# The first half of the fourth 1/den load, moved ahead of three LN2 transposes in the DMA queue

## Chip, cores, metric

One NeuronCore of one Trainium2 chip. The metric is the device time of one execution in microseconds (us).

## The reference, cut

One transformer block on 2048 tokens of width 1024: a modulated layernorm, a linear attention with 32 heads, a second modulated layernorm (LN2) and a GEGLU feed-forward network (FFN) of width 3584. What matters here:

```python
num = einsum(pq, kv);  den = einsum(pq, z) + 1e-6
o = num / den                                   # 1/den per token and head
x = x + ga * (o @ wo)                           # "x1"
h = layernorm(x) * (1 + cb) + sb                # LN2
x = x + gb * ((gelu(h @ w_gate) * (h @ w_up)) @ w_down)
```

## The kernel before

Tokens go in 16 tiles of 128, in four groups of 512. The 1/den of a group is computed once, stored to DRAM and loaded back spread over partitions: two halves for each group, each of four loads of 256 KB. The queries `pq` are multiplied by it on VectorE, then TensorE makes the attention output of one tile after another (`wo_chunk`). Groups share two buffers, so the fourth group's load overwrites the second's.

```python
def rb_load(sg, hs=(0, 1)):
    i = sg % 2                                   # buffer
    for h in hs:
        for k in range(HPG):                     # four loads of 256 KB
            sch.dma(Q, ... RB[i][32*k:32*(k+1), h] <- scr_rd[sg, h, k] ...)
...
def ln2_a(c_, late):                             # LN2 of one tile (cut)
    ln_stats_act(c_, b_, rng, 0); ln_stats_act(c_, b_, rng, 1)
    xhat_act(c_, b_, rng)                        # ScalarE: normalized tile
    tdma(Q, H2[sg][...], b_[:, :], ...)          # DMA transpose into h2T
...
ln2_a(0, False)
stream_pair(0, 0)                                # FFN weights: gate, up (512 KB each)
for c_ in range(3, 12):
    if c_ == 3: pq_scale(1, 0, GH[0] + GH[1])
    if c_ == 4: pq_scale(1, 1, GH[0] + GH[1])
    wo_chunk(c_, 2 * (c_ % 4))
    ...
    if c_ == 9:
        stream_pair(0, 1)
        rb_load(3, (1,))
        x_dma(12, 16)
    if c_ in (10, 11): pq_scale(3, 0, GH[c_ - 10])
    if c_ in (4, 5, 6): ln2_a(c_ - 3, False)     # tiles 1, 2, 3
    if c_ == 6: rb_load(3, (0,))                 # <- this moves
    if c_ == 9: mod2(0, 2); mod2(2, 2)           # VectorE: scale and shift of h2T
stream_pair(0, 2)
```

All these DMAs are issued by one engine, SP, in program order; SP waits before each for whatever that DMA needs. The first FFN matmuls need a modulated block of h2T from all four tiles 0 to 3. Tiles count from 0: the transposes of tiles 1, 2 and 3, called transposes 1, 2 and 3, are those of the second, third and fourth tile.

## Time and profile before

| | before |
|---|---|
| median of 3 runs (range), us | 834.2 (833.83 to 834.79) |
| span of the profiled execution, us | 832.2 |
| TensorE busy | 99% |
| third up-weights: issued, landed, us | 238.58, 252.44 |
| TensorE hole there (start to start less the usual 0.216) | 0.588 us |
| first FFN matmul, us | 234.42 |

The first 190 us jitter between executions. Where tenths matter I therefore count from the start of the first attention-output matmul (191.22 us here): "to the end" is the end of the span less that start, 641.00 us in this profile. Steps between matmul starts and DMA landings are from the trace's own instruction and semaphore records; the views print durations and rounded starts.

### The profile page before, as it was taken

The page shows a single profiled execution, that of the slowest core. Times are in us where ns is not written, and L with a number is a line of the kernel's source. Part 1 is how long each engine was busy: PE and PEld are TensorE (multiplying, and loading weights), DVE is VectorE, ACT ScalarE, POOL GpSimd, SP SyncE. Part 2 cuts the span into 40 slices and gives each one's busy share as a digit, 9 for nine tenths or more (in the row PEclk, how much of TensorE's full clock was granted, in tenths as well). Part 3 has the DMA queues.
Part 4 walks back from the last instruction along what each step waited for, and adds up shares of the span by engine and source line. Part 5 has one row for each costly group of instructions (what it writes and reads, how often), then busy time and mean ns, then how long its engine had stood idle before and what let it go on. Part 6 is the DMA issues. An engine that isn't in the chain of part 4 may idle for free.

```text
span 832.2 us, 11518 instructions
## 1 busy us (share of the span) xinstructions
PE 821.7 (99%) x4179; PEld 391.9 (47%) x4253; DVE 509.7 (61%) x920; ACT 321.3 (39%) x542; POOL 36.2 (4%) x90
## 2 busy tenths in 40 slices
PE   8999999999999999999999999999999999999998
PEld 4444446665444444444444444444444444444445
DVE  6799888834776577753555565355556535555522
ACT  2597642323523354410444441044444104444300
POOL 2122200000200000000000000000000000000000
PEclk9999999999999999999999999999999999999999
DMA  9788769358999789170555533065553306555000
GB/s 288 230 182 223 166 136 274 48 121 195 205 254 289 227 244 262 31 173 19 158 153 152 151 102 76 20 163 152 154 146 102 76 20 171 155 152 137 7 20 26
DMA packets 216929, 121.90 MB, mean 146 GB/s; under 512 B 69276, under 2 KB 206756, under 8 KB 215848
## 3 DMA queue, kind: packets, MB, share of 16 engines
q1 hardware_dynamic: 216856, 121.16, 56.1%
q8 instruction: 34, 0.56, 0.3%
q14 instruction: 23, 0.19, 0.1%
q10 hardware_dynamic: 16, 0.00, 0.0%
HBM read 103.03 MB, written 4.47 MB: 129 GB/s over the span
## 4 chain that ended last, share of the span: by engine, by line
PE 92%; SPq 3%; DMA 3%; issue 1%; DVE 1%; ACT 0%; ACTq 0%
PE ps_all L1359 23%; PE ps_all L1334 22%; PE ps_all L1331 21%; PE ps_all L826 7%; PE ps_all L862 7%; PE ps_all L811 5%; PE ps_all L1193 5%; DMA wu<-in_B_w_up_dram 2%; SPq L568 1%; DMA wmq<-in_w_mod_dram 1%; SPq L1172 1%; SPq L573 1%; PE ps_all L844 0%; PE ps_all L1121 0%; SPq L562 0%
## 5 line engine op out<-in xcount | busy, mean ns | idle before, releaser
L1334 PE MATMUL ps_all<-h2T,wu 128*128 128x512 bf16 x896 | 339.6, 379 | 2.3 <-DMA wu<-in_B_w_up_dram 0.4
L1331 PE MATMUL ps_all<-h2T,wg 128*128 128x512 bf16 x860 | 325.9, 379 | 0.0
L1359 PE MATMUL ps_all<-wd,yT 128*128 128x512 bf16 (+3 forms) x934 | 193.1, 366 | 0.9
L1342 ACT ACTIVATE q<-ps_all 128x512 f32<-128x512 f32 x112 | 66.9, 597 | 222.3 <-PE ps_all L1331 217.1
L1359 PEld LDWEIGHTS ps_all<-wd,yT 128*128 128x128 bf16 x952 | 90.1, 98 | 103.7 <-issue 0.2
L1334 PEld LDWEIGHTS ps_all<-h2T,wu 128*128 128x128 bf16 x896 | 87.7, 98 | 106.5 <-DMA wu<-in_B_w_up_dram 0.9
L1331 PEld LDWEIGHTS ps_all<-h2T,wg 128*128 128x128 bf16 x896 | 87.7, 98 | 105.6
L1347 DVE SCALAR_TENSOR_TENSOR ww<-th,guh 128x512 f32<-128x512 f32 x112 | 77.5, 692 | 77.9 <-ACT th L1346 77.9
L1344 DVE SCALAR_TENSOR_TENSOR ww<-q,ps_all 128x512 f32<-128x512 f32 x112 | 76.9, 687 | 74.5 <-ACT guh L1343 74.3
L1346 ACT ACTIVATE th<-ww 128x512 f32<-128x512 f32 x112 | 70.5, 629 | 87.5 <-DVE ww L1344 87.5
L1364 DVE TENSOR_TENSOR ps_all<-ps_all,gbb 128x512 f32<-128x512 f32 (+3 forms) x34 | 22.7, 667 | 94.6 <-PE ps_all L1359 94.6
L1349 DVE TENSOR_TENSOR yT<-ww,ps_all 128x512 bf16<-128x512 f32 x112 | 76.9, 686 | 3.8
L1343 ACT ACTIVATE guh<-ps_all 128x512 f32<-128x512 f32 x112 | 66.3, 592 | 0.0
L862 PE MATMUL ps_all<-h1T,wq 128*128 128x512 bf16 x256 | 56.7, 379 | 0.0
L1193 PE MATMUL ps_all<-w,pq 128*128 128x512 bf16 x252 | 56.3, 379 | 0.2
L811 PE MATMUL ps_all<-wk,h1T 128*128 128x512 bf16 x239 | 55.3, 379 | 1.2 <-DMA wk<-in_A_wqkv_dram 0.5
L800 ACT ACTIVATE eb<-ps_all 128x512 f32<-128x512 f32 x64 | 36.4, 593 | 38.1 <-PE ps_all L811 14.8
L862 PEld LDWEIGHTS ps_all<-h1T,wq 128*128 128x128 bf16 x256 | 25.0, 98 | 29.9
L1193 PEld LDWEIGHTS ps_all<-w,pq 128*128 128x128 bf16 x256 | 24.9, 98 | 30.0 <-ACT w L1123 0.3
L811 PEld LDWEIGHTS ps_all<-wk,h1T 128*128 128x128 bf16 x248 | 23.6, 97 | 28.9 <-DVE h1T L691 2.3
L826 PE MATMUL ps_all<-xall,pk 128*128 128x342 bf16 (+1 forms) x216 | 35.2, 307 | 0.0
L630 ACT ACTIVATE xhd<-xall,nm,rs 128x1024 bf16<-128x1024 bf16 x12 | 14.9, 1240 | 38.2 <-DVE nm L620 31.7
(97 smaller groups left out, 506.6 us busy)
## 6 DMA issues: line engine op xcount, KB each, us to landing
wg<-in_B_w_gate_dram SPq DMA_DIRECT2D x56, 512.0 KB, 3.9
wu<-in_B_w_up_dram SPq DMA_DIRECT2D x56, 512.0 KB, 5.2
rb<-scr_rd SPq DMA_DIRECT2D x32, 256.0 KB, 5.8
wd<-in_B_w_down_dram SPq DMA_DIRECT2D x7, 1024.0 KB, 8.9
wmst<-in_w_mod_dram SPq DMA_DIRECT2D x6, 1024.0 KB, 6.4
wmq<-in_w_mod_dram SPq DMA_DIRECT2D x8, 512.0 KB, 7.5
out_dram<-xall SPq DMA_DIRECT2D x31, 128.0 KB, 1.7
xall<-in_A_x_dram SPq DMA_DIRECT2D x3, 1024.0 KB, 9.1
```

What stands on the lines that cost most here:

```text
L811: o = sch.op(T, lambda e, dc=dc: e.matmul(PS(bank), H1[sg][:, ci, dc, :], W_[:, dc, jg * 512:(jg + 1) * 512], start=(dc == 0), stop=(dc == ...
L826: o = sch.op(T, lambda e, c_=c_: e.matmul(PS(bank, 0, n), PK[c_][:, g * P:(g + 1) * P], xrow(c_, o_, o_ + n), start=(c_ == 0), stop=(c_ == ...
L862: o = sch.op(T, lambda e, dc=dc: e.matmul(PS(b), WQ[:, dc, qc * P:(qc + 1) * P], H1[sg][:, :, dc, :], start=(dc == 0), stop=(dc == NDC - 1 ...
L1193: last[half] = sch.op(T, lambda e, g=g, half=half: e.matmul(PS(b0 + half), PQ[sg][:, g, ci * P:(ci + 1) * P], W2[:, g, half * 512:(half + ...
L1331: og = sch.op(T, lambda e, dc=dc: e.matmul(PS(bg), WG[slot][:, dc, e_ * P:(e_ + 1) * P], H2[sg][:, dc, :], start=(dc == 0), stop=(dc == ND ...
L1334: ou = sch.op(T, lambda e, dc=dc: e.matmul(PS(bu), WU[slot][:, dc, e_ * P:(e_ + 1) * P], H2[sg][:, dc, :], start=(dc == 0), stop=(dc == ND ...
L1342: sch.op(A, lambda e: e.activation(Q1[j][:, :], PS(bg), ACTF.Square, scale=math.sqrt(GELU_A)), prd=pr(bg), wr=rq, note=f"q1 {fc}")
L1344: sch.op(V, lambda e: e.scalar_tensor_tensor(WW[j][:, :], Q1[j][:, :], 1.0, PS(bg), op0=ALU.add, op1=ALU.mult), rd=rq, prd=pr(bg), wr=rw, ...
L1346: sch.op(A, lambda e: e.activation(TH[j][:, :], WW[j][:, :], ACTF.Tanh, scale=GELU_C), rd=rw, wr=rt, note=f"th {fc}")
L1347: sch.op(V, lambda e: e.scalar_tensor_tensor(WW[j][:, :], TH[j][:, :], 1.0, GUH[j][:, :], op0=ALU.add, op1=ALU.mult), rd=rt + rg, wr=rw, n ...
L1349: sch.op(V, lambda e: e.tensor_tensor(YT[:, fc, :], WW[j][:, :], PS(bu), ALU.mult), rd=rw, prd=pr(bu), wr=r_yt(fc), note=f"yT {fc}")
L1359: o = sch.op(T, lambda e, b=b, fc=fc, c0=c0, c1=c1, n=n: e.matmul(PS(b, 0, n), YT[:, fc, ci * P:(ci + 1) * P], WDT[fc // 4][:, fc % 4, c0:c1],
```

## The change

Its intent: issue the half-load earlier, while the queue still has nothing to wait for. It now precedes the transposes of tiles 1, 2 and 3 instead of following them.

```diff
             if c_ == 4:
                 pq_scale(1, 1, GH[0] + GH[1])
+                rb_load(3, (0,))
             wo_chunk(c_, 2 * (c_ % 4))
...
             if c_ in (4, 5, 6):
                 ln2_a(c_ - 3, False)
-            if c_ == 6:
-                rb_load(3, (0,))
```

## The prediction

> **What bounds the kernel now.** I read the busy shares first, then the chain that ended last, then who made TensorE wait between 170 and 300 us (the stretch that the change touches), then the order of time of TensorE, the DMA queue (SP) and VectorE there, and last the DMA share in slices of 2 us.
>
> ```profile
> PE 821.7 (99%) x4179; PEld 391.9 (47%) x4253; DVE 509.7 (61%) x920; ACT 321.3 (39%) x542; POOL 36.2 (4%) x90
> PE 92%; SPq 3%; DMA 3%; issue 1%; DVE 1%; ACT 0%; ACTq 0%
> ```
>
> TensorE is the bound: 99% busy and 92% of the last chain. From 24 us to the end it issues one 128x512 matmul about every 216 ns. A change can help only where TensorE has a hole. The waits of TensorE from 170 to 300 us are one line, and the order of time shows the place:
>
> ```profile
> PE ps_all L1334 <- DMA wu<-in_B_w_up_dram: 0.4, 1, 0.4
> ...
> 251.69 0.38 PE L1331 MATMUL ps_all<-h2T,wg 128*128 128x512 bf16 x1
> 252.49 0.39 PE L1334 MATMUL ps_all<-h2T,wu 128*128 128x512 bf16 x1 [0.42 <-DMA wu<-in_B_w_up_dram]
> 252.72 0.38 PE L1331 MATMUL ps_all<-h2T,wg 128*128 128x512 bf16 x1
> ```
>
> The first up-matmul of the third FFN weight pair starts 804 ns after its predecessor (start times in the trace) instead of 216: 588 ns are lost. The other odd steps of this stretch, 432 ns every 10.79 us, are exactly two steps and recur to the end, so I take them for missing records. The chain says what stands behind the hole:
>
> ```profile
> 220.28 8.42 SPq L670 DMA_TRANSPOSE h2T<-xh  x3
> 228.79 1.94 SPq L1172 DMA_DIRECT2D rb<-scr_rd  x4
> 230.83 0.39 SPq L1271 DMA_DIRECT2D wg<-in_B_w_gate_dram  x1
> 231.32 0.53 SPq L1272 DMA_DIRECT2D wu<-in_B_w_up_dram  x1
> 231.90 5.56 SPq L1172 DMA_DIRECT2D rb<-scr_rd  x4
> 237.50 0.42 SPq L562 DMA_DIRECT2D xall<-in_A_x_dram  x1
> 238.03 0.45 SPq L1271 DMA_DIRECT2D wg<-in_B_w_gate_dram  x1
> 238.58 5.05 SPq L1272 DMA_DIRECT2D wu<-in_B_w_up_dram  x1
> ```
>
> This is the DMA queue: three LN2 transposes (tiles 1 to 3), the four loads that the change moves, second weight pair, second half of the fourth 1/den load, x, third weight pair. Its last load is issued at 238.58 and lands 13.9 us later, at 252.4. In the trace's semaphore records 15 of its 16 increments come at 250.88 to 250.99 and the last at 252.44: one DMA engine was held by a 16 KB instruction fetch that starts at 243.78 and takes 1.36 us. Yet the DMA engines had a hole of their own earlier (last two columns: DMA share, GB/s):
>
> ```profile
> 224.00:226.00 2.00, 2.00 (x11) 0.88 (x9) 1.74 (x2) 0.65 (x2) 1.03 (x3) 1.00 1.27 285
> 226.00:228.00 2.00, 2.00 (x11) 0.94 (x10) 0.97 (x3) 1.24 (x1) 0.13 (x1) 1.00 0.04 8
> 228.00:230.00 2.00, 2.00 (x11) 0.93 (x10) 2.00 (x6) 0.00 (x0) 0.00 (x0) 1.00 1.04 120
> ```
>
> At 226 to 228 us they stand still: the queue is blocked by the fourth transpose's wait for its normalized tile,
>
> ```profile
> SPq L1476 <- ACT xh L630: 2.7, 1, 2.7
> ```
>
> and all behind it waits along, though the moved load has been ready since 207.7 us, when the last scaling that reads its old buffer ends on VectorE.
>
> **What the Trainium skill says.** "DMA: Bandwidth & Descriptors", section "Queues, rings and completion order": each DMA engine consumes descriptors in ring order. The trace agrees: landings of this queue come in issue order. The same page, "Rules for kernel authors": a transpose next to ordinary DMAs needs nothing, so I expect no draining around the transposes; in the trace the packets of the first transpose overlap those of x and of the first weight pair between 218 and 221 us. "Perfetto Trace Analysis", section "DMA Instruction — HWDGE (DVE, Sync)": the window shown for a DMA instruction is descriptor generation, not movement. The trace agrees: the last load above shows 5.05 us and lands after 13.9. "DMA: Bandwidth & Descriptors", "Why a DMA increments its semaphore by 16 and not by 1": only the full 16 means landed, which is why the one late engine at 252.44 counts.
>
> **The change part by part.** Four loads of 256 KB (1 MB) move in the DMA queue from behind transpose 3 to ahead of transpose 1. No instruction of TensorE, VectorE, ScalarE or GpSimd changes its place: the kernel's reordering step covers an earlier segment. Nothing is added.
>
> Costs on the DMA engines, from packets and landings before: the four loads land 1.2 us apart (232.71, 233.96, 235.12, 236.32), so 4.7 us for all four; a weight pair takes 3.6 us; a transpose about 1 us.
>
> Forward from the landing of the first weight pair, 224.9, unchanged: the moved loads land until 224.9 + 4.7 = 229.6. Transposes 1 and 2 landed at 225.7 and 226.5 and now land near 230.6 and 231.4. Transpose 3 is still ready only after its tile at 227.4, and landed at 231.27; it now stands behind a busy queue and lands near 232.4, about 1.1 us later: 4.7 us of added load less the hole, the issue delay behind it and the load no longer sharing engines with it.
>
> Who needs it: VectorE modulates 8 blocks for tiles 0 and 1, then 8 for tiles 2 and 3:
>
> ```profile
> 228.85 2.13 DVE L691 TENSOR_SCALAR h2T<-h2T,cb1T,sbT 128x256 bf16<-128x256 bf16 x8
> 231.37 2.14 DVE L691 TENSOR_SCALAR h2T<-h2T,cb1T,sbT 128x256 bf16<-128x256 bf16 x8 [0.39 <-DMA h2T<-xh]
> ```
>
> The first eight move to about 230.7 to 232.8 (transpose 1), the second to 232.8 to 235.0. The first FFN matmul starts at 234.42 and needs one modulated block of all four tiles: ready at 232.8 + 0.3 = 233.1, so 1.3 us remain of a slack that was 2.8. VectorE makes a block in 0.27 us and TensorE uses one in 0.43, so later blocks stay ahead. This beginning costs nothing. The x1 addition of tile 10 follows at about 235.0 to 236.2; its banks are wanted at 241.3 by the third hidden block. The scaling that waited 1.8 us for the moved load at 236.44 waits no longer and VectorE catches up by 240.
>
> Behind transpose 3 the queue is 3 us or so ahead: second pair 236.1 (before 239.9; wanted at about 241), second half of the load 240.9, x 243.5, third pair 247.2, with the 1.45 us of the fetch 248.7. That is 3.7 us before 252.4 and 3.2 before TensorE wants it (251.69 + 0.22 = 251.9). I keep 2.5 to 3.7 as my range for the advance; 0.6 suffices. The hole of 0.588 us closes. Sum: 834.2 - 0.6 = 833.6. All after it runs at TensorE's pace with no other DMA wait, so the gain is kept but cannot grow: the other 3 us that the DMA gains meet no waiting engine.
>
> **The rivals.** First: the transposes come too late and the hole moves to 234.42. SP's issue may be blocked by a full queue (the first half-load at 231.90 needed 4.16 us, and transpose 1 2.67). If transposes 2 and 3 are issued only when the moved loads are nearly done, near 228.7, transpose 3 lands at 228.7 + 3.8 = 232.5: still in time. If transpose 1 lands 1.5 us later than I say, each further us costs nearly one: 834.2 to 835.2. For it speaks the saturated queue; against it the 1.3 us of slack. Chance 15%.
>
> Second: the load is hidden either way and the third pair lands no earlier, as SP is blocked elsewhere: 834.2. Its issue waits are back-pressure, which an emptier queue reduces, so I give it 10%.
>
> Third: a large gain, as the DMA queue is full for 40 us. Against it: TensorE lost only 0.588 us to DMA here, and this is the ceiling unless the trace hides more. Under 2%.
>
> Fourth: the earlier second pair lets TensorE start the FFN sooner. No: it issues the last attention-output matmul immediately before 234.42, without a gap.
>
> **Range and chances.** Centre 833.6. The three runs before span 833.83 to 834.79, about half a us to either side, as large as the effect. With the gain and that scatter 832.9 to 834.1; with the first rival up to 834.6. I say 832.9 to 834.6. Over 2% would be 16.7 us; nothing here is of that size. Faster 0.5%, same 99%, slower 0.5%.
>
> **What would show it.** Right: no DMA wait of TensorE near 252; start to start there back at 216 ns; the 226 to 228 slice full of 8 KB packets (220 GB/s instead of 8); transpose 3 landing at 232 to 233; second modulation starting near 232.8; third up-weights landing before 250; VectorE's waits for the 1/den load down from 6.0 us to about 4.2; span near 831.6. Wrong: a TensorE wait on VectorE's modulation at 234.4, or transpose 3 landing after 234, or the up-weight wait still there.

## The result, and the profile after

| | before | after |
|---|---|---|
| median, us, 6 runs each | 833.95 | 833.83 |
| range, us | 833.53 to 834.79 | 833.48 to 835.07 |
| ratio, 95% interval | | 1.000 (0.9987 to 1.0012) |
| profiled span, us | 832.2 | 832.4 |
| first attention-output matmul to the end, us | 641.00 | 640.61 |

A ratio is the mean time of one kernel's fast runs over the mean of the other's in the same rounds, so not quite the ratio of these medians. The times alone show no difference: the interval spans 2.1 us, over three times the 0.6 us that were predicted. The trace is finer. First the page after, its busy line and the engines of its last chain (the two FFN matmul lines are now L1330 and L1333, one up from before):

```profile
PE 825.4 (99%) x4253; PEld 391.6 (47%) x4253; DVE 509.5 (61%) x920; ACT 321.2 (39%) x542; POOL 36.7 (4%) x90
PE 97%; SPq 1%; DMA 1%; issue 0%; DVE 0%
```

The chain no longer runs back through the DMA queue at 252 us (SP and DMA had 3% each before); it stays on TensorE. The waits of TensorE from 170 to 300 us are now an empty list: the hole at the third up-weights is closed. In the order of time of TensorE, however, a small new step stands at the first FFN matmul:

```profile
232.83 2.32 PE L1193 MATMUL ps_all<-w,pq 128*128 128x512 bf16 x10
235.19 0.38 PE L1330 MATMUL ps_all<-h2T,wg 128*128 128x512 bf16 x1
```

Its start is 411 ns after its predecessor's instead of 216, so 195 ns are lost; the view marks no idle time, since ends of matmuls are modelled and overlap. (This profile holds all 4253 matmuls, the one before 4179, and here no step of 432 ns recurs: those of the prediction were missing records, as it took them.) What feeds it is seen on SP, in VectorE's waits and VectorE's order of time, and in the DMA share (last two columns of the last line):

```profile
221.73 2.18 SPq L1172 DMA_DIRECT2D rb<-scr_rd  x4
224.02 8.25 SPq L670 DMA_TRANSPOSE h2T<-xh  x3
232.36 0.53 SPq L1271 DMA_DIRECT2D wg<-in_B_w_gate_dram  x1
...
DVE h2T L691 <- DMA h2T<-xh: 3.1, 1, 3.1
...
232.65 4.19 DVE L691 TENSOR_SCALAR h2T<-h2T,cb1T,sbT 128x256 bf16<-128x256 bf16 x16 [3.14 <-DMA h2T<-xh]
...
226.00:228.00 2.00, 2.00 (x11) 0.91 (x10) 1.26 (x3) 0.61 (x1) 1.19 (x3) 1.00 1.25 262
```

The DMA hole at 226 to 228 us is filled, 262 GB/s instead of 8. But VectorE now waits 3.1 us for the transposes, where it waited 0.4, and the run of 16 modulations starts only at 232.65. Of the three transposes the first takes 1.24 us to issue, the second 5.54, and the third only starts at 231.02 (trace records). They land at 232.21, 233.04 and 234.41.

Sum for this pair of profiles, counted to the end: -0.588 (old hole) + 0.195 (new step) = -0.393; measured 640.61 - 641.00 = -0.39. That the span is 0.2 us longer all the same comes from before the change: the first attention-output matmul started 0.57 us later (191.79 against 191.22).

### The profile page after: what moved, and what is told of

The parts are those of the page before. It is cut to its first block, busy times and chain, and to the rows that moved or that the text cites. A ratio compares the mean times of both kernels' runs of the same rounds, so it can differ in the third digit from the quotient of the medians.

```text
span 832.4 us, 11591 instructions
## 1 busy us (share of the span) xinstructions
PE 825.4 (99%) x4253; PEld 391.6 (47%) x4253; DVE 509.5 (61%) x920; ACT 321.2 (39%) x542; POOL 36.7 (4%) x90
## 4 chain that ended last, share of the span: by engine, by line
PE 97%; SPq 1%; DMA 1%; issue 0%; DVE 0%
PE ps_all L1358 23%; PE ps_all L1330 23%; PE ps_all L1333 23%; PE ps_all L826 7%; PE ps_all L862 7%; PE ps_all L1193 7%; PE ps_all L811 6%; DMA wmq<-in_w_mod_dram 1%; SPq L568 1%; PE ps_all L844 0%; SPq L573 0%; PE ps_all L1121 0%; SPq L562 0%; PE ps_all L1152 0%; PE ps_all L728 0%; PE ps_all L771 0%
## 5 line engine op out<-in xcount | busy, mean ns | idle before, releaser
L1330 PE MATMUL ps_all<-h2T,wg 128*128 128x512 bf16 x896 | 339.6, 379 | 0.0
L1333 PE MATMUL ps_all<-h2T,wu 128*128 128x512 bf16 x896 | 339.6, 379 | 0.0
L1330 PEld LDWEIGHTS ps_all<-h2T,wg 128*128 128x128 bf16 x896 | 87.7, 98 | 106.1 <-issue 0.5
L1333 PEld LDWEIGHTS ps_all<-h2T,wu 128*128 128x128 bf16 x896 | 87.7, 98 | 105.6
```

The costliest lines, as they stand in the source:

```text
L1330: og = sch.op(T, lambda e, dc=dc: e.matmul(PS(bg), WG[slot][:, dc, e_ * P:(e_ + 1) * P], H2[sg][:, dc, :], start=(dc == 0), stop=(dc == ND ...
L1333: ou = sch.op(T, lambda e, dc=dc: e.matmul(PS(bu), WU[slot][:, dc, e_ * P:(e_ + 1) * P], H2[sg][:, dc, :], start=(dc == 0), stop=(dc == ND ...
```

## The experiments

Two theories stood at the start. Mine: the gain is the closed hole, and its price is a step at the first FFN matmul, because the transposes, now behind 1 MB, land so late that VectorE's modulation sets the start of the FFN. The rival: both are jitter of the DMA queue, or the step is something else. All twelve runs gave correct results.

This table holds what the trace records of every profile say. Times in the first columns count from the first attention-output matmul. "9th modulation" is the first of the second eight, the one that completes a block of h2T for all four tiles; "step" and "hole" are the excess over 0.216 us.

| profile | 9th modulation starts | first FFN matmul | step there | hole at third up-weights | to the end |
|---|---|---|---|---|---|
| before | 40.15 | 43.20 | 0 | 0.588 | 641.00 |
| e1 (before) | 40.17 | 43.20 | 0 | 0.619 | 641.04 |
| e11 (before) | 40.15 | 43.20 | 0 | 0.316 | 640.74 |
| after | 42.91 | 43.39 | 0.195 | 0 | 640.61 |
| e2 (after) | 43.48 | 43.97 | 0.773 | 0 | 641.18 |
| e8 (after) | 42.22 | 43.20 | 0 | 0 | 640.41 |
| e9 (after) | 42.80 | 43.29 | 0.094 | 0 | 640.50 |
| e10 (after) | 42.83 | 43.32 | 0.125 | 0 | 640.53 |
| e3 | 42.74 | 43.23 | 0.034 | 0 | 640.44 |
| e4 | 47.76 | 48.25 | 5.056 | 0 | 647.43 |
| e5 | 42.36 | 43.20 | 0 | 0 | 640.41 |
| e6 | 40.15 | 43.20 | 0 | 0 | 640.41 |
| e7 | 39.91 | 43.20 | 0 | 0 | 640.41 |
| e12 | 40.10 | 43.20 | 0 | 0 | 640.41 |

### e1: the kernel before again

Edit: none.

> The kernel before, run again as a control. Measure: in the profile, the time from the start of the first attention-output matmul to the end of the span, which leaves out the jitter of the first 190 us. It was 641.00 us before and 640.61 after the change. My theory (a hole of 0.588 us at the third up-weights is closed, a new one of 0.195 us opens at the first FFN matmul): again 641.0, with one step of about 0.8 us at 252 us and no step at the first FFN matmul. Rival (both holes are jitter of the DMA queue and come and go from run to run): the step at 252 is absent or of another size, 640.4 to 641.5. Time ratio to the same kernel 1.000 in both.

Measured: 833.87 us, ratio 1.0003 (0.9989 to 1.0017). The hole is there again, 0.619 us, and no step at the FFN's start; 641.04. The late last increment of the third up-weights is there too, 250.93 for fifteen and 252.40 for the last. The hole is thus not an accident of one execution.

### e2, e8, e9, e10: the changed kernel again

Edit: none against the changed kernel.

> The changed kernel again. My theory: first attention-output matmul to end 640.6 (0.4 less than before), the step at 252 gone, a step of 0.3 to 0.6 us (instead of 0.216) at the first FFN matmul because transposes 2 and 3 land near 233 and 234.4. Rival (jitter of the upstream DMA alone made the transposes late in the one profile): no step at the first FFN matmul, 640.4. Time: 0.4 us less than before, 0.9995, which an interval of about 0.1% will hardly tell from 1.

> The changed kernel a third time, for its profile. The two profiles so far had a step of 0.411 and 0.989 us at the first FFN matmul (0.216 is none), and 640.61 and 641.18 us from the first attention-output matmul to the end. My theory: a step between 0.3 and 1.1 us again, the sum 640.4 plus what the step is over 0.216. Rival (the step is a rare accident): no step.

> The changed kernel again, on one chip with a run of the kernel before and of the best variant. In the three profiles of it so far the second 1/den load's last part was issued 17.9 to 18.2 us after the first attention-output matmul, and 17.3 to 17.5 us in the seven profiles of the other kernels, although nothing differs between them up to there; the step at the first FFN matmul was 0.411, 0.989 and 0.216 us. Theory A (run-to-run jitter upstream of the change decides whether the step opens): the 17.9 to 18.2 and the step do not always appear; the sum from the first attention-output matmul to the end is 640.4 plus whatever the step is over 0.216. Theory B (the changed kernel always lags there): 17.9 to 18.2 again. Time 0.2 to 0.5 us less than before.

> As the fourth look: theory A, jitter: any value from 17.3 to 18.2 and a step from none (0.216) to 1.0 us; theory B: 17.9 to 18.2. The sum 640.4 to 641.2, 640.4 plus the step over 0.216.

Measured: e2 833.49 us, ratio 0.9996 (0.9983 to 1.0010); e9 833.45, ratio 0.9996 (0.9982 to 1.0009); e8 and e10 one run each, 833.44 and 833.50. The hole at 252 us is gone in all. The step varies: 0.773, 0, 0.094 and 0.125 us beside the 0.195 above. In e2 it is large enough for the waits of TensorE (170 to 300 us) and its order of time to name it; VectorE's lines show why:

```profile
PE ps_all L1330 <- DVE h2T L691: 0.6, 1, 0.6
...
234.80 0.38 PE L1330 MATMUL ps_all<-h2T,wg 128*128 128x512 bf16 x1 [0.61 <-DVE h2T L691]
...
231.95 2.14 DVE L691 TENSOR_SCALAR h2T<-h2T,cb1T,sbT 128x256 bf16<-128x256 bf16 x8 [3.40 <-DMA h2T<-xh]
234.31 2.14 DVE L691 TENSOR_SCALAR h2T<-h2T,cb1T,sbT 128x256 bf16<-128x256 bf16 x8 [0.23 <-DMA h2T<-xh]
```

Here the second eight modulations even wait once more, for the transpose of tile 3 (landed 234.21), and TensorE's first FFN matmul follows 0.49 us behind the first of them. My expectation for e2 held in direction, not in size (641.18 against 640.6); that for e8 failed, there was no step.

The table has the rule: the first FFN matmul starts at 43.20 us, when the attention output is done, or 0.49 us after the 9th modulation, whichever is later. It fits all of the changed kernel's five profiles within 0.01 us. Which transpose holds the 9th modulation back differs. In the profile after the change it is transpose 1, landed at 40.42 by the common count: the first eight modulations start at 40.85 and the second eight follow without a wait. In e2, e8, e9 and e10 it is transpose 3, landed at 43.38, 42.12, 42.70 and 42.73: the 9th modulation starts 0.10 us later.

What varies lies upstream of the change: the first weight pair lands at 34.7, 35.1, 33.8, 34.3 and 34.5 in the five, in the order of the table, and the steps rank as these landings do. What moves that landing is not shown. The last of the eight loads of the third group's 1/den (the expectation of e9 calls it the second 1/den load's last part) does not do it alone: it is issued 17.98, 17.88, 18.22, 17.90 and 18.22 us after the first attention-output matmul, so the largest step comes with the earliest issue, and no step with one of the two latest.

### e3: the load ahead of the fourth transpose alone

```diff
+            if c_ == 6:
+                rb_load(3, (0,))
             if c_ in (4, 5, 6):
                 ln2_a(c_ - 3, False)
-            if c_ == 6:
-                rb_load(3, (0,))
```

> The half-load is put ahead of the fourth transpose alone, so transposes 1 and 2 keep their place and the load fills the queue's wait for the fourth tile. My theory: transposes 1 and 2 land as before (5.4 and 3.5 us after issue), the fourth near 232.5 to 233.5; first modulation not delayed, second starts near 233; no step at the first FFN matmul and none at 252: first attention-output matmul to end 640.4. Rival (any load ahead of the fourth transpose delays the FFN's start): a step at the first FFN matmul as in the changed kernel, 640.6. Time 0.6 us less than before.

Measured: 833.59 us, ratio 0.9998 (0.9986 to 1.0011); 640.44. SP, VectorE and the DMA share:

```profile
220.01 4.41 SPq L670 DMA_TRANSPOSE h2T<-xh  x2
224.52 1.92 SPq L1172 DMA_DIRECT2D rb<-scr_rd  x4
227.14 1.23 SPq L670 DMA_TRANSPOSE h2T<-xh  x1
...
228.53 2.13 DVE L691 TENSOR_SCALAR h2T<-h2T,cb1T,sbT 128x256 bf16<-128x256 bf16 x8
233.63 2.14 DVE L691 TENSOR_SCALAR h2T<-h2T,cb1T,sbT 128x256 bf16<-128x256 bf16 x8 [2.98 <-DMA h2T<-xh]
...
226.00:228.00 2.00, 2.00 (x11) 0.88 (x9) 0.97 (x2) 1.08 (x1) 0.00 (x0) 1.00 0.85 205
```

The transposes of tiles 1 and 2 are issued at once and the first eight modulations are on time; the load fills the queue's wait for the fourth tile, and the hole at 252 us is gone. The fourth transpose lands at 233.53, the second eight modulations start at 42.74 by the table's count, and the rule gives 43.23: a step of 0.034 us. The place is right but has no slack left.

### e4: the suspected cost enlarged

```diff
                 rb_load(3, (0,))
+                rb_load(3, (1,))
...
-                rb_load(3, (1,))
```

> Both halves of the fourth 1/den load (2 MB instead of 1) ahead of the second tile's transpose: the suspected cost enlarged. My theory (the transposes land behind the loads and VectorE's modulation of them sets the FFN's start): another 4.7 us on each transpose, so the first FFN matmul is 4.5 to 5 us later, in one step of about 5 us; nothing of it is given back, first attention-output matmul to end 645 to 646, time near 838.5. Rival (the transposes are not what starts the FFN, the 0.195 us step is something else): under 1 us of step, time unchanged.

Measured: 840.33 us, ratio 1.0079 (1.0065 to 1.0092). The step came as expected, 5.06 us, and its releaser is named; the time came out 1.8 us worse than the 838.5 I expected, slower by 0.8% and clear of 1. TensorE's order of time, then the slice after the step (the third number from the end is the granted clock):

```profile
239.75 0.58 PE L1330 MATMUL ps_all<-h2T,wg 128*128 128x512 bf16 x1 [4.89 <-DVE h2T L691]
240.13 0.63 PE L1333 MATMUL ps_all<-h2T,wu 128*128 128x512 bf16 x1
240.55 0.63 PE L1330 MATMUL ps_all<-h2T,wg 128*128 128x512 bf16 x1
...
239.70:244.00 4.30, 4.25 (x11) 1.56 (x12) 4.30 (x11) 0.00 (x0) 0.00 (x0) 0.53 1.09 327
```

The trace's clock records have the granted clock at 0.5 from 236.93 to 243.76 (0.53 is the mean of the slice), so after the idle 5 us the first 4 us of matmuls ran at half clock and started every 427 ns instead of 216: eight of those, and two partial ones, add 1.96 us. The Trainium skill has this, in "TensorE: Matmul & The Clock Gate", section "What's actually happening": after an idle window of about 3.4 us the clock falls to half until the array has been busy for about as long. This run agrees in kind and on the busy side: the clock rose 4.0 us after the first FFN matmul (239.75). It fell sooner than that, 2.1 us after the modelled end of the last attention-output matmul (234.86). Sum: 640.41 + 5.06 + 1.96 = 647.43, as measured. So what is put ahead of the transposes does set the start of the FFN; the rival that the step is something else falls.

### e5: the load between the second and third tile's transpose

```diff
+            if c_ == 5:
+                rb_load(3, (0,))
             if c_ in (4, 5, 6):
                 ln2_a(c_ - 3, False)
-            if c_ == 6:
-                rb_load(3, (0,))
```

> The half-load between the second tile's transpose and the third's. What is to be told apart: does one transpose behind the four loads go into the queue at once and a second one wait until the loads are nearly through (so in the changed kernel: transpose 1 took 1.2 to 1.6 us to issue, transpose 2 5.5 to 5.7), or are all delayed by the load's 4.7 us alike? If the queue holds the loads and one transpose: transpose 1 lands as before (about 5.4 us after issue), transpose 2 is issued at once, the issue of transpose 3 ends only near the landing of the last moved load, and it lands near 233.5; step at the first FFN matmul 0.2 to 0.5 us. Rival (only the order on the engines counts): transpose 3 issued at once after its tile. Time 0.3 to 0.6 us less than before, 640.4 to 640.7 from the first attention-output matmul to the end.

Measured: 833.36 us, ratio 0.9998 (0.9984 to 1.0011); 640.41, no step. The first transpose behind the loads issued in 1.23 us, the second in 2.90: its issue ended at 230.18, the last moved load landed at 230.74. In the changed kernel it ended at 230.91 with the landing at 231.47. So one transpose goes in behind the four loads at once and a second only when the loads are nearly through, half a us before the last of them lands; the rival, issue at once, falls. Whether the second waits for the loads, or for the transpose before it to begin, these runs do not tell apart. The second landed at 233.29 as expected, but without the step of 0.2 to 0.5 us that I expected with it: by the rule the 9th modulation at 42.36 leaves 0.35 us.

### e6: another way to close the hole

```diff
                 rb_load(3, (1,))
-                x_dma(12, 16)
...
         stream_pair(0, 2)
+        x_dma(12, 16)
```

The half-load stays where it was before.

> The kernel before with its half-load where it was, but with the load of the last four x tiles behind the third weight pair instead of ahead of it. My theory (the hole at 252 us is only the third pair's place in the queue): the third up-weights land 2.5 us earlier, near 250 with the late engine, the step at 252 us is gone, the transposes and the FFN's start are as before: 640.4. The last x tiles land near 252 to 253 and are first read at about 254.4, so no new wait of TensorE. Rival (the hole would go to another load or to the x1 addition): a wait of TensorE between 250 and 290 us. Time 0.6 us less than before.

Measured: 833.63 us, ratio 0.9998 (0.9984 to 1.0012); 640.41, no wait of TensorE between 170 and 300 us. The third up-weights land at 249.94 and TensorE's order of time passes the place without a stop:

```profile
251.89 0.38 PE L1331 MATMUL ps_all<-h2T,wg 128*128 128x512 bf16 x1
252.11 0.38 PE L1334 MATMUL ps_all<-h2T,wu 128*128 128x512 bf16 x1
```

The hole was only the third pair's place in the queue, and it can be closed without touching the transposes.

### e7 and e12: two of the four loads moved

```diff
-def rb_load(sg, hs=(0, 1)):
+def rb_load(sg, hs=(0, 1), ks=range(HPG)):
...
+                rb_load(3, (0,), (0, 1))         # ahead of the second tile's transpose
...
-                rb_load(3, (0,))
+                rb_load(3, (0,), (2, 3))         # behind the fourth, as before
```

> Of the four loads only two (512 KB) go ahead of the second tile's transpose, the other two stay behind the fourth. My theory (cost by the amount ahead of the transposes): transposes 1 and 2 land about 2.4 us later than before instead of 4.7 to 6, the fourth near 232, no step at the first FFN matmul; the third pair lands 1.5 to 2.5 us earlier than before, hole at 252 gone: 640.4. Rival (any load ahead of the transposes costs the same, for instance by the order of issue): a step of 0.2 to 0.8 us as in the changed kernel.

> The variant with two of the four loads ahead of the transposes, timed in five rounds: its first profile had slack at both places (second modulation ready 3 us before the first FFN matmul, third up-weights landed 2 us before their matmul). Expected: 640.4 us from the first attention-output matmul to the end, no step; time 0.3 to 0.6 us less than the kernel before, ratio 0.9993 to 0.9997, which the interval will not tell from 1. If it beats the changed kernel at all, then by 0 to 0.8 us.

Measured: e7 833.32 us, ratio 0.9997 (0.9983 to 1.0010); e12 833.30, ratio 0.9995 (0.9983 to 1.0008); 640.41 both times. SP and VectorE in e7:

```profile
220.50 1.26 SPq L1172 DMA_DIRECT2D rb<-scr_rd  x2
221.87 6.91 SPq L670 DMA_TRANSPOSE h2T<-xh  x3
228.83 1.03 SPq L1172 DMA_DIRECT2D rb<-scr_rd  x2
...
228.93 4.42 DVE L691 TENSOR_SCALAR h2T<-h2T,cb1T,sbT 128x256 bf16<-128x256 bf16 x16
```

The fourth transpose lands at 231.11, as early as before, and VectorE's 16 modulations run through without a wait. The third up-weights land at 249.88. In e12 the upstream lag of the changed kernel's profiles was there too (17.90 us) and no step came of it. By its slack at both places (2.8 us at the first FFN matmul and 2.1 us at the third up-weights in e7, 2.6 and 1.9 in e12) it stands with e6 (2.6 and 2.2, and 2.0 for the x tiles, which land at 252.75 and are read at 254.71) ahead of the other variants. By time it is not shown to beat the changed kernel: in e9 and e12 their medians are 833.45 and 833.30.

### e11: the kernel before a third time

Edit: none.

> The kernel before a third time, on this chip. Theory A: 17.3 to 18.2 us here too, no step at the first FFN matmul even if it lags (slack 2.8 us), the step of about 0.8 us at the third up-weights again: 641.0. Theory B: 17.3 to 17.5.

Measured: 833.72 us, one run. The hole was 0.316 us this time, because the third up-weights landed 0.27 us earlier by the common count (60.95 against 61.22; the last three of the 16 increments came at 250.98, 251.20 and 252.15). The upstream start was 17.67 us, between the two groups seen so far. The changed kernel had come out as theory B says (17.90 and 18.22), but e7 and e12, one kernel, gave 17.48 and 17.90, and e4, whose kernel is the changed one with more moved, gave 17.51; these speak for theory A: the lag is jitter, not a property of the changed kernel. Why all five profiles of the changed kernel lie at 17.88 or above stays open.

## Why the prediction was right or wrong

The time was inside the range, but that proves little: the kernel before lies inside the same range (833.95), and the medians differ by 0.12 us, not 0.6. The centre of 833.6 was optimistic, and one part of the sum was mis-sized.

Of the signs that the prediction named, four came: no DMA wait near 252 us, 216 ns from start to start there, the full slice at 226 to 228 us, and VectorE's waits for 1/den down from 6.0 to 4.1 us. Four did not: transpose 3 landed at 234.41 (said 232 to 233; "after 234" was a sign of being wrong), the second modulation started at 234.70 (said 232.8), the third up-weights landed at 251.18 (said before 250), and the span was 832.4 (said 831.6). The later start of 0.57 us explains part of each, but not the whole. And the wait of TensorE on the modulation, another sign of being wrong, is named in e2 (0.6 us).

- TensorE bounds, and DMA can win only the hole: right. Every variant without a hole or step takes 640.41 us to the end, and none takes less.
- "The hole of 0.588 us closes": right, in five of five profiles. The hole itself was not a constant: 0.588, 0.619 and 0.316 us in three profiles of the kernel before, so on average about 0.51 was there to win.
- "This beginning costs nothing": this is the step that failed. Measured, it cost 0.195, 0.773, 0, 0.094 and 0.125 us, on average 0.24. The first rival, given 15%, came true in four of five profiles, in small size.
- The terms under it. Transpose 1 was put at 230.6, or 39.4 by the common count; it landed at 39.6 to 40.7. Transpose 3 was put about 1.1 us later than before; by the common count it landed at 42.1 to 43.4 against 40.05, so 2.1 to 3.3 later. Two things were left out. I held transposes 1 to 3 to a smooth stream of 1 us each, though I named the blocked issue as a risk: transpose 2 was blocked 5.5 us and transpose 3 issued behind it (e5 shows that the block ends with the moved loads). And I took the first weight pair's landing at 224.9 as fixed, where upstream jitter moved it by 0.1 to 1.4 us. The allowance from modulation to matmul was 0.3 us, measured 0.49. Together the 1.3 us of slack became -0.8 to +0.5 us.
- "3 us or so ahead" for the third pair: 1.2 to 2.4 us by the common count. The shortfall has a second part besides the late transposes: in the changed kernel the increments of the second weight pair are spread over 2.3 to 2.9 us (237.79 to 240.07 in the first profile), where before they came within 0.1. Its cause stays open. It did not matter, 0.6 us was enough.
- Sum from the profiles' means: 0.24 - 0.51 = -0.27 us, not -0.6. The times agree without proving it: e2 and e9 each came out at 0.9996 with intervals that hold 1, and the first comparison at 1.000.
- The second and third rivals, no earlier landing and a large gain, did not occur. The fourth, an earlier start of the FFN, could not: 43.20 us is set by TensorE's own work.
- Two readings of the prediction go too far, without harm to its sum. The 216 ns from start to start hold from about 190 us on; from 24 to 190 us narrower matmuls lie between, and the median step is 148 ns. And that the late engine at 252.44 was held by an instruction fetch is not shown (see the last section).

## What to carry to other kernels

When a DMA queue stands still behind an instruction that waits for its data, put a ready transfer into that wait, and no more than leaves the blocked instruction its slack: all of it directly ahead of the blocked instruction left none (e3, a step of 0.034 us), half of it, even at the earliest place, left 2.6 us and more (e7, e12), and all of it at the earliest place cost up to 0.77 us. The wait was 2.7 us; two loads take about 2.4 us, four 4.7. What is put ahead and outlasts the wait delays what the next stage starts with. Or move another transfer behind the late one (e6). All this is read from the traces; by time no variant but e4 is shown to differ from the kernel before. Before moving a transfer, name both consumers, the one that gains and the one behind which it cuts in, and compare the slack of both with the jitter of the queue, not with a single profile. And a hole that is made large enough costs more than itself: after 5 us of idleness TensorE restarted at half clock (e4).

## What the Trainium skill lacked or had wrong

- "DMA: Bandwidth & Descriptors" and "Perfetto Trace Analysis" give no depth for the queue of issued DMAs. Here a DMA transpose issued in 1.23 us when there was room (e3); behind four loads of 256 KB the first took 1.2 to 1.6 us (the changed kernel, e2, e5, e8 to e10) and the second 5.5 to 5.7 (2.9 in e5, where it came later), ending 0.3 to 0.6 us before the last of those loads landed (the changed kernel, e2, e5). What is counted, descriptors, bytes or instructions, these runs do not tell.
- What an instruction fetch costs the data transfers beside it is not given; its place would be "Runtime: NRT & Kernel Launch". In this stretch packets of 16 KB on the instruction queue took 1.0 to 1.4 us. One of 1.36 us at 243.78 fits the last of 16 increments of a weight load, 1.45 us late (250.99, then 252.44), and so the hole that this change was for. That it was the cause is not shown: the records name no DMA engine, and in e5 the last increment came 1.58 us late (248.04, then 249.62) with a packet of 1.04 us.
- "DMA: Bandwidth & Descriptors", section "Rules for kernel authors", says of a transpose next to ordinary DMAs that it needs nothing. The row is about wrong data, and so far it holds: all runs were correct. Of time it says nothing, and here the transposes' place in the queue decided up to 0.77 us in the changed kernel and 5.06 us in e4.
- "TensorE: Matmul & The Clock Gate", section "What's actually happening", gives about 3.4 us for both the fall and the rise of the clock. In e4 the clock fell 2.1 us after TensorE's last matmul ended and rose 4.0 us after the next began.
